# Second FFN stage: sums of blocks ahead of the other item's low part on VectorE, and 18 shared tiles

## The chip, the cores and the metric

One core of one Trainium2 chip runs the whole program. The time is device microseconds (us) of one execution; the kernel before takes 1112.65 us, the median of 3 runs (1112.34 to 1115.46).

## The reference

Sigmoid attention and a two-layer network behind it, in float32:

```python
scores = scale * np.matmul(q, k.transpose(0, 1, 3, 2)) - np.log(S)
attn = 1.0 / (1.0 + np.exp(-scores))
out = np.matmul(attn, v)              # 8 batches, 12 heads, 448 x 64
x = out.transpose(0, 2, 1, 3).reshape(B * S, H * D)      # 3584 x 768
h = x @ w_in                          # w_in 768 x 2048
g = np.maximum(0.01 * h, h)
return g @ w_out                      # w_out 2048 x 768
```

## The kernel before, in words

The program has three parts: attention, the first FFN product and the second FFN product. The change lies in the second product (`acc_*` on TensorE), and in the last slots of the first, where its work begins.

**Two parts for one number.** TensorE multiplies float32 numbers in a rounded form. So each operand is split: a high part (ScalarE copies it into the rounded type) and a low part (VectorE subtracts the high part from the whole). Three matmuls, high by high, high by low and low by high, stand for one product.

**Phases and items.** Tokens are worked in four phases p (two batches, 2 x 448 tokens each). The second product is a bilinear scheme: blocks of the activations g are combined, multiplied by combined blocks of w_out (20 "forms"), and the 20 products are summed up in 6 result tiles. The table `PRODUCTS` (line 41 on) has one entry for each product: its form of the weights, its accumulator chain in PSUM (A, B, D, E or C), its operand, and what is read out behind it. An operand such as `"30"` or `"01+30"` that the first stage has stored as a block of its own (`RAW`, `MADE`) is "single": it is loaded and split. One such as `"21-30"` that is not stored is a sum: both blocks are loaded, and VectorE adds or subtracts them. Singles are products 0, 2, 3, 4, 5, 7, 8, 10, 11 and 19, sums are 1, 6, 9 and 12 to 18. Each product is worked in two halves of two 128-row blocks: `items` has 4 x 20 x 2 = 160 entries (p, i, h). An item is 12 matmuls of 128 x 448. Within a phase, product i is items 2i and 2i + 1.

**Readouts.** `read` follows a product's second half: `"c10"` copies the accumulator to a new result tile (ScalarE), `"r11"`, `"+21"` and `"-00"` add it to or subtract it from a result tile or the other way round (VectorE). `!` marks the last change of a result, whose store to DRAM follows one slot later. A phase has 6 copies by ScalarE and 11 readouts by VectorE; two of these follow product 14.

**Order.** Each engine carries out its instructions in the order in which the program issues them (`pinned`). The program advances in slots: `slot(work)` first runs what was put off to this slot (`later`), then the work. In the second stage, slot k issues for VectorE and ScalarE the preparation of later items, and for TensorE the 12 matmuls of item k (the second of them is the first that reads the low part). Before the change, the order in slot k is: readouts of the product that ended with item k - 1 (k even) and stores that fell due; weights (`Wide`) that are loaded on the way, mainly in phase 0: 21 loads, each with a high part two slots later and a low part three slots later; then

```python
g_low(k + 1)      # VectorE: low part of item k+1
g_sum(k + 2)      # VectorE: sum of item k+2, over the block loaded last
g_high(k + 2)     # ScalarE: high part of item k+2
g_load(k + 4)     # SyncE: loads of item k+4
```

So on VectorE the sum of item k + 2 is followed directly by the low part of that same item (in slot k + 1), which reads what ScalarE makes out of the sum in between; where a readout falls due, it stands between them.

**Tiles.** Blocks are loaded into a ring of 6 tiles `g` (128 x 896 float32, 3.5 KB in a partition), high and low parts are made in a ring of 3 double tiles `gs`, results lie in a ring of 6 tiles `o`. An instruction that is the first to write a tile waits for whatever used that tile last. A block that two neighbouring products share is loaded once unless a sum has been written over it. Loads and stores are all issued by SyncE, in order.

Of the kernel before, what the change touches and what calls it, by code (L numbers as in the profile page):

```python
# [9 lines left out]
F32 = mybir.dt.float32  # L10
# [6 lines left out]
P = 128  # L17
# [6 lines left out]
PLACES = slice(1, 3), slice(3, 5), slice(5, 7), slice(0, 1)  # L24
ST = 10
AHEAD = 7
GG = 6

PACES = (4, 5, 4.2, 2.8, 2), 2.7
WAIT = 7  # L30
# [17 lines left out]
BLOCKS = "02", "01", "10", "00", "21", "03", "22", "11", "12", "13", "20", "23"  # L48
FORMS = 20
TRIPLES = tuple(range(i, min(i + 3, FORMS)) for i in range(0, FORMS, 3))  # L50
# [17 lines left out]
def attn_ffn_kernel(ctx: ExitStack, tc: tile.TileContext, qk, v, w_in, w_out, out):  # L68
# [41 lines left out]
    def sub(to, x, y):  # L110
        vec(out=to, in0=x, in1=y, op=ALU.subtract)
# [10 lines left out]
    def later(slots, *fns, first=False):  # L122

        chores.setdefault(now + slots, ([], []))[not first].extend(fns)

    def slot(work=None):
        nonlocal now
        for fns in chores.pop(now, ()):
            for fn in fns:
                fn()  # L130
        if work is not None:
            work()
        now += 1
# [644 lines left out]
        product(NQ - 1, first, k)  # L778
    right.close()
    KS = 2  # L780
    gp = ctx.enter_context(tc.tile_pool(name="gp", bufs=3, side="right", reuse_waits="tile"))
    shift(ctx, "pad2", 64, "right")
    t2a = ctx.enter_context(tc.tile_pool(name="t2a", bufs=AHEAD, side="right", reuse_waits="tile"))
    more = ExitStack()
    w1_stage.extend([more.enter_context(tc.tile_pool(name="stage2", bufs=4, side="right", reuse_waits="tile"))])

    items = [(p, i, h) for p in range(NQ) for i in range(FORMS) for h in range(2)]
    raw, gx, gs = {}, {}, {}

    def operand(x):  # L790

        fn = add if "+" in x else sub
        return (fn, *x.replace("-", "+").split("+"))

    def g_load(k):
        if k >= len(items):
            return
        p, i, h = items[k]
        x = PRODUCTS[i][2]
        names = [x] if x in gd[p] else operand(x)[1:]  # L800
        mine = []
        for n in names:
            if raw.get((p, n, h), -9) < k - 2:
                t = gp.tile([P, KS, S], F32, tag="g", name=f"g{n[:2]}_{p}_{i}_{h}", bufs=GG)
                dma(out=t, in_=gd[p][n][:, h * KS:h * KS + KS])
                raw[p, n, h], gx[p, n, h] = k, t
                mine.append(n)
        gs[k] = [None, mine[-1]]

    def g_sum(k):  # L810
        if k >= len(items):
            return
        p, i, h = items[k]
        x = PRODUCTS[i][2]
        gs[k][0] = gx[p, gs[k][1], h]
        if x not in gd[p]:
            fn, a, b = operand(x)
            fn(gs[k][0], gx[p, a, h], gx[p, b, h])
            del raw[p, gs[k][1], h]

    def g_high(k):
        if k < len(items):
            gs[k].append(gp.tile([P, 2, KS, S], F32R, tag="gs", name="gs{}_{}_{}".format(*items[k])))
            copy(out=gs[k][2][:, 0], in_=gs[k][0])

    def g_low(k):
        if k < len(items):
            sub(gs[k][2][:, 1], gs[k][0], gs[k][2][:, 0])

    use = [(g, u) for g in range(len(TRIPLES)) for u in range(KQ)]  # L830
    w2 = {(g, u): Wide(g, u, t2a, "t2") for g, u in use[:AHEAD]}
# [1 line left out]
    for k in range(NOP, size):  # L833
        m, at = divmod(k - NOP, 6)
        if m < AHEAD:
            x = w2[use[m]]
            if at == 1:
                later(0, x.load)
                later(3, x.high)
                later(4, x.low)  # L840
        rest = size - k
        if rest <= 4:
            later(0, lambda r=rest: g_load(4 - r))
        if rest == 2:
            later(0, lambda: g_sum(0), lambda: g_high(0))
        elif rest == 1:
            later(0, lambda: g_low(0), lambda: g_sum(1), lambda: g_high(1))
        slot(first.step)
    while chores:
        slot()  # L850
# [1 line left out]
    more.close()  # L852
    left.close()

    op = ctx.enter_context(tc.tile_pool(name="op", bufs=6, reuse_waits="tile"))
    t2b = ctx.enter_context(tc.tile_pool(name="t2b", bufs=len(use) - KQ - AHEAD - len(GROUPS), reuse_waits="tile"))
    for i, (g, u) in enumerate(use[AHEAD:]):
        small = len(TRIPLES[g]) < 3
        pool, tag = (ring, "ring") if i < len(GROUPS) else (t2b, "t1" if small else "t2")
        w2[g, u] = Wide(g, u, pool, tag, KQ if small else None)  # L860
# [6 lines left out]
    def place(p, o):  # L867
        m, t = int(o[0]), int(o[1])
        b = 2 * p + t
        return out[2 * m:2 * m + 2, :, b * S:(b + 1) * S]  # L870

    def store(p, o):
        dma(out=place(p, o).rearrange("m p s -> p m s"), in_=outs[p, o])

    def read(p, i):
        _, chain, _, reads = PRODUCTS[i]
        acc = accs[p, chain][:, :, :S]
        for x in reads:
            how, o = x[0], x[1:3]
            if how == "c":  # L880
                outs[p, o] = op.tile([P, 2, S], F32, tag="o", name=f"o{p}_{o}")
                copy(out=outs[p, o], in_=acc)
            else:
                t = outs[p, o]
                a, b = (acc, t) if how == "r" else (t, acc)
                (add if how == "+" else sub)(t, a, b)
            if x[3:]:
                later(1, lambda o=o: store(p, o))
# [5 lines left out]
    for k, (p, i, h) in enumerate(items):  # L894
        form, chain, _, reads = PRODUCTS[i]
        begins = h == 0 and firsts_at[chain] == i
        if begins:
            accs[p, chain] = psum("acc", f"acc{p}_{chain}")
        ending = k == len(items) - 1
        def work():  # L900
            for far, step in ((3, "low"), (2, "high"), (0, "load")):
                for x in loads.get(k - far, ()):
                    getattr(x, step)()
            g_low(k + 1)
            g_sum(k + 2)
            g_high(k + 2)
            g_load(k + 4)
            x = gs.pop(k)[2]
            g = form // 3
            for m in range(2):  # L910
                todo = [(e, part, n) for e in range(KS) for part, n in ((0, 0), (0, 1), (1, 0))]
                for at, (e, part, n) in enumerate(todo):
                    mm(accs[p, chain][:, m, :S], lhsT=w2[g, h * KS + e].of(form, part, m), rhs=x[:, n, e],
                       start=begins and at == 0, stop=h == 1 and at == len(todo) - 1, skip_group_check=True)
                if ending:

                    o, = (x[1:3] for x in reads)
                    t, acc, to = outs[p, o], accs[p, chain], place(p, o)
                    for cols, queue in zip(HALVES, (dma, dma_act)):
                        add(t[:, m, cols], t[:, m, cols], acc[:, m, cols])  # L920
                        queue(out=to[m, :, cols], in_=t[:, m, cols])

        slot(work)
        if h == 1 and not ending:
            later(0, lambda p=p, i=i: read(p, i))
    while chores:
        slot()
    ps.close()
# [42 lines left out]
```

## Time and profile before

| what | value |
|---|---|
| median of 3 runs | 1112.65 us |
| the profiled execution, its own time | 1114.31 us |
| its span, first to last instruction | 1112.5 us |
| granted TensorE clock, mean | 0.998 |
| TensorE busy (matmuls) | 1062.9 us, 96% |
| VectorE busy | 828.1 us, 74% |
| ScalarE busy | 607.1 us, 55% |
| moved by DMA | 298.61 MB, mean 268 GB/s |

Shares of the whole span hide what each part does. TensorE's matmuls overlap, and the ends of matmuls are modelled, so a busy share of 96% does not mean that it runs at its peak; how far apart matmuls start tells more. The chain of work that ended last puts 69% of the span on TensorE, 16% on VectorE, 6% on ScalarE and 6% on issuing. In the lines of the profile "idle before, releaser" is the time in which an engine stood still ahead of an instruction, and what ended it.

### The profile page before, as it was taken

Reading aid. Unit: us, or ns where it says so; the run is one execution under the profiler, and the core shown is the slowest. Engines: PE = TensorE matmul, PEld = TensorE weight load, DVE = VectorE, ACT = ScalarE, POOL = GpSimd, SP = SyncE. Lnnn points to the kernel's source line nnn. Section 1 sums busy time; section 2 is a strip of 40 time slices with the busy share of each in tenths; the row PEclk is TensorE's granted clock in tenths of the full one; section 3 lists DMA queues with packets and bytes.
Section 4 is the critical chain, followed back from the end, with each engine's and each line's share of the span. In section 5 each row is a group of like instructions: output and inputs, shape, how many; then the busy total and the mean of one; then the engine's idle time right before and its main releaser. Section 6 shows DMA issues by size and latency. Waiting matters only on the chain.

```text
span 1112.5 us, 16285 instructions
## 1 busy us (share of the span) xinstructions
PE 1062.9 (96%) x5786; PEld 867.3 (78%) x5786; DVE 828.1 (74%) x1187; ACT 607.1 (55%) x829; POOL 0.3 (0%) x5
## 2 busy tenths in 40 slices
PE   9999999999999999999999999979998899889987
PEld 5554555558999998998999988868886789678966
DVE  4778899777897889789675667887567756766675
ACT  6877877785556555655565546643442344334422
POOL 0000000000000000000000000000000000000000
PEclk9999999999999999999999999999999999999999
DMA  7878887897889798998887889888767876786675
GB/s 249 275 276 280 302 280 257 308 307 227 265 282 308 245 310 275 295 347 259 272 273 249 267 298 347 307 283 283 227 217 234 292 224 210 239 294 227 206 244 197
DMA packets 128000, 298.61 MB, mean 268 GB/s; under 512 B 13488, under 2 KB 66736, under 8 KB 127920
## 3 DMA queue, kind: packets, MB, share of 16 engines
q1 hardware_dynamic: 127200, 296.90, 80.0%
q8 instruction: 45, 0.74, 0.3%
q10 hardware_dynamic: 720, 0.69, 0.2%
q14 instruction: 35, 0.29, 0.1%
HBM read 210.89 MB, written 86.64 MB: 267 GB/s over the span
## 4 chain that ended last, share of the span: by engine, by line
PE 69%; DVE 16%; ACT 6%; issue 6%; DMA 1%; ACTq 0%; DVEq 0%; SPq 0%
PE px_h L103 18%; PE pv L103 11%; PE sc L103 10%; PE pz_h L103 9%; PE acc_A L103 8%; DVE g L103 7%; PE acc_B L103 6%; ACT gs L103 6%; DVE gs L103 5%; PE py_h L103 4%; PE acc_C L103 2%; DVE w L103 1%; DMA wx<-t 1%; DVE s L103 1%; PE acc_D L103 1%
## 5 line engine op out<-in xcount | busy, mean ns | idle before, releaser
L103 ACT CAST gs<-g 128x896 fp32r<-128x896 f32 x160 | 149.0, 942 | 242.0 <-DVE g L103 199.9
L103 DVE TENSOR_TENSOR gs<-g,gs 128x896 fp32r<-128x896 f32 x160 | 172.6, 1089 | 89.7 <-ACT gs L103 88.8
L103 PE MATMUL px_h<-hi,w 128*128 128x448 f32 x768 | 232.1, 363 | 3.0 <-DVE w L103 3.0
L103 PEld LDWEIGHTS px_h<-hi,w 128*128 128x128 f32 x768 | 143.3, 187 | 15.7 <-DVE w L103 5.5
L103 PE MATMUL px_h<-lo,w 128*128 128x448 f32 x384 | 139.1, 362 | 0.0
L103 PE MATMUL acc_B<-gs,w 128*128 128x448 f32 x576 | 122.2, 364 | 4.8 <-DVE gs L103 4.8
L103 PE MATMUL acc_A<-gs,w 128*128 128x448 f32 x576 | 121.6, 364 | 4.8 <-DVE gs L103 4.8
L103 ACT ACTIVATE s<-sc 128x896 f32<-128x896 f32 x144 | 119.5, 933 | 10.2 <-PE sc L103 10.2
L103 PEld LDWEIGHTS acc_B<-gs,w 128*128 128x128 f32 x576 | 107.1, 188 | 16.0 <-DVE gs L103 8.9
L103 PEld LDWEIGHTS acc_A<-gs,w 128*128 128x128 f32 x576 | 107.2, 187 | 15.4 <-DVE gs L103 8.2
L103 PE MATMUL pz_h<-hi,w 128*128 128x448 f32 x384 | 118.1, 362 | 0.0
L103 PE MATMUL pv<-s,v 128*64 128x448 f32 x576 | 114.0, 544 | 0.0
L103 DVE TENSOR_TENSOR w<-wx,w 128x768 fp32r<-128x768 f32 (+1 forms) x128 | 109.0, 853 | 6.2 <-ACT w L103 6.2
L103 PEld LDWEIGHTS sc<-qks 64*128 64x128 f32 x876 | 80.8, 189 | 24.1 <-issue 16.9
L103 PE MATMUL sc<-qks 64*128 64x448 f32 (+1 forms) x876 | 96.6, 371 | 0.5 <-DVE x L103 0.3
L103 ACT CAST w<-wx 128x768 fp32r<-128x768 f32 (+1 forms) x128 | 95.9, 750 | 0.3
L103 PEld LDWEIGHTS pv<-s,v 128*64 128x64 f32 x576 | 39.2, 137 | 64.2 <-issue 54.2
L103 DVE TENSOR_TENSOR g<-g,g 128x896 f32<-128x896 f32 x80 | 86.8, 1085 | 0.0
L103 PE MATMUL acc_D<-gs,w 128*128 128x448 f32 x288 | 67.5, 377 | 16.1 <-DVE gs L103 16.1
L103 ACT COPY c_h<-px_h 128x448 f32<-128x448 f32 x64 | 34.2, 534 | 89.0 <-PE px_h L103 79.9
L103 PEld LDWEIGHTS px_h<-lo,w 128*128 128x128 f32 x384 | 72.0, 188 | 4.8
L103 PEld LDWEIGHTS pz_h<-hi,w 128*128 128x128 f32 x384 | 72.0, 187 | 4.8
(61 smaller groups left out, 1323.1 us busy)
## 6 DMA issues: line engine op xcount, KB each, us to landing
g<-g SPq DMA_DIRECT2D x208, 448.0 KB, 4.2
wx<-t SPq DMA_DIRECT2D x96, 384.0 KB, 4.4
g<-c_h SPq DMA_DIRECT2D x128, 224.0 KB, 4.5
g<-s SPq DMA_DIRECT2D x96, 224.0 KB, 4.5
qk<-in_qk SPq DMA_DIRECT2D x46, 448.0 KB, 5.5
wr<-in_w_in SPq DMA_DIRECT2D x32, 384.0 KB, 3.3
wr<-in_w_out SPq DMA_DIRECT2D x32, 384.0 KB, 3.8
out<-o SPq DMA_DIRECT2D x23, 448.0 KB, 4.5
```

The source lines that it names most:

```text
L103: return lambda *args, **kw: tc.keep_in_program_order(issue(*args, **kw))
```

## The change

- **Order on VectorE.** In slot k the sum of item k + 2 now stands in front of the low part of item k + 1 (before: behind it); the high part of item k + 2 on ScalarE follows as before. Where a sum shares a block with the single product just before it (products 1 and 9), it is made one slot earlier still, since that single's low part is written over the block. Readouts move from the front of the slot behind the sums, the low parts and the weights.
- **Tiles.** Rings are given up. 18 tiles of one size (12 of `gp`, 6 of `op`) are handed out one by one from a list, the one given back longest ago first, for loaded blocks, sums, high parts and results alike. A low part is written over a loaded block of its own, a high part over the second one where there is one, else into a new tile. A sum gets a new tile, given back after the item's low part.
- **Loads.** An item is loaded when enough tiles are spare, up to 8 items ahead of the one whose matmuls were issued last (before: 4); `wanted` keeps tiles back for what the next slot needs. The loads of a slot are issued at its end. Product 16 is written `31+01`, and product 17 shares its block 31, so that a phase has 50 loads of blocks (before: 52).
- **Start.** The first item is loaded one slot earlier, and the sum of item 2 is made in the last slot of the first stage, in front of the low part of item 0.
- `op` now lies behind the weights `t2b` in memory.

```diff
--- before.py
+++ after.py
@@ -24,7 +24,7 @@
 PLACES = slice(1, 3), slice(3, 5), slice(5, 7), slice(0, 1)
 ST = 10
 AHEAD = 7
-GG = 6
+GG, OO, FAR = 12, 6, 8
 
 PACES = (4, 5, 4.2, 2.8, 2), 2.7
 WAIT = 7
@@ -44,7 +44,7 @@
     (4, "A", "01", ("r21",)), (5, "B", "10-21", ("c01",)), (6, "A", "10+01", ("c20",)), (7, "B", "21-20", ("c00",)),
     (8, "A", "10", ("r00",)), (9, "B", "20-10", ()), (10, "A", "11-10", ("r01",)), (11, "B", "00+30", ("r10!",)),
     (12, "D", "01-00", ("-00!",)), (13, "E", "11+01", ()), (14, "C", "30-31", ("-01!", "-21")), (15, "D", "30-20", ()),
-    (17, "C", "01+31", ()), (19, "E", "21-31", ("+21!",)), (18, "D", "10+00", ("-20!",)), (16, "C", "11-21", ("+11!",)))
+    (17, "C", "31+01", ()), (19, "E", "21-31", ("+21!",)), (18, "D", "10+00", ("-20!",)), (16, "C", "11-21", ("+11!",)))
 BLOCKS = "02", "01", "10", "00", "21", "03", "22", "11", "12", "13", "20", "23"
 FORMS = 20
 TRIPLES = tuple(range(i, min(i + 3, FORMS)) for i in range(0, FORMS, 3))
@@ -778,54 +778,116 @@
         product(NQ - 1, first, k)
     right.close()
     KS = 2
-    gp = ctx.enter_context(tc.tile_pool(name="gp", bufs=3, side="right", reuse_waits="tile"))
+    gp = ctx.enter_context(tc.tile_pool(name="gp", bufs=1, side="right", reuse_waits="tile"))
     shift(ctx, "pad2", 64, "right")
     t2a = ctx.enter_context(tc.tile_pool(name="t2a", bufs=AHEAD, side="right", reuse_waits="tile"))
     more = ExitStack()
     w1_stage.extend([more.enter_context(tc.tile_pool(name="stage2", bufs=4, side="right", reuse_waits="tile"))])
 
     items = [(p, i, h) for p in range(NQ) for i in range(FORMS) for h in range(2)]
...
+    spare, homes = [(gp, f"g{n}") for n in range(GG)], {}
+
+    def grab(name, dtype=F32R):
+
+        pool, tag = spare.pop(0)
+        t = pool.tile([P, KS, S], dtype, tag=tag, name=name)
+        homes[id(t)] = pool, tag
+        return t
+
+    def drop(t):
+        spare.append(homes.pop(id(t)))
+
+    class Operand:
+
+        def __init__(self, k):
+            self.k = k
+            self.p, self.i, self.h = items[k]
+            x = PRODUCTS[self.i][2]
+            self.single = x in gd[self.p]
+            self.names = [x] if self.single else x.replace("-", "+").split("+")
+            self.fn = add if "+" in x else sub
+            self.before = operands[k - 2] if self.i else None
+            self.shared = [n for n in self.names if self.before and n in self.before.new] if not self.single else []
+            self.new = [n for n in self.names if n not in self.shared]
+            self.lent, self.made, self.hi, self.ready = (), None, None, False
+            if self.before:
+                self.before.lent = self.shared
+
+        def label(self, what):
+            return f"{what}_{self.p}_{self.i}_{self.h}"
+
+        def load(self):
+            self.raw = {}
+            for n in self.new:
+                t = self.raw[n] = grab(self.label(f"g{n[:2]}"))
+                dma(out=t.bitcast(F32), in_=gd[self.p][n][:, self.h * KS:self.h * KS + KS])
+
+        def first(self):
+
+            return self.before and self.before.single and self.shared
+
+        def whole(self):
+            if self.ready:
+                return
+            self.ready = True
+            if self.single:
+                self.lo, = self.raw.values()
+                self.x = self.lo.bitcast(F32)
+                return
+            a, b = (self.before.raw[n] if n in self.shared else self.raw[n] for n in self.names)
+            self.made = self.x = grab(self.label("gf"), F32)
+            self.fn(self.made, a.bitcast(F32), b.bitcast(F32))
+            if self.shared and not self.before.single:
+                for n in self.shared:
+                    drop(self.before.raw[n])
+            own = [t for n, t in self.raw.items() if n not in self.lent]
+            self.lo = own.pop()
+            self.hi = own.pop() if own else None
+
+        def high(self):
+            if self.hi is None:
+                self.hi = grab(self.label("gh"))
+            copy(out=self.hi, in_=self.x)
+
+        def low(self):
+            sub(self.lo, self.x, self.hi)
+            if self.made is not None:
+                drop(self.made)
+
+        def done(self):
+            drop(self.hi)
+            drop(self.lo)
+
+    operands = []
+    for k in range(len(items)):
+        operands.append(Operand(k))
+    ahead = 0
+
+    def wanted(k):
+
+        n = 0
+        for j in (k + 2, k + 3):
+            x = operands[min(j, len(items) - 1)]
+            n += not x.single and (j == k + 2 or bool(x.first())) and not x.ready
+        x = operands[min(k + 2, len(items) - 1)]
+        n += x.single or len([m for m in x.new if m not in x.lent]) < 2
+        if k and k % 2 == 0:
+            n += sum(y[0] == "c" for y in PRODUCTS[items[k - 1][1]][3])
+        return n
+
+    def g_load(k, far):
+
+        nonlocal ahead
+        while ahead <= min(far, len(items) - 1) and len(spare) >= len(operands[ahead].new) + wanted(k + 1):
+            operands[ahead].load()
+            ahead += 1
+
+    def g_step(k, step):
         if k < len(items):
-            gs[k].append(gp.tile([P, 2, KS, S], F32R, tag="gs", name="gs{}_{}_{}".format(*items[k])))
-            copy(out=gs[k][2][:, 0], in_=gs[k][0])
-
-    def g_low(k):
-        if k < len(items):
-            sub(gs[k][2][:, 1], gs[k][0], gs[k][2][:, 0])
+            getattr(operands[k], step)()
 
     use = [(g, u) for g in range(len(TRIPLES)) for u in range(KQ)]
     w2 = {(g, u): Wide(g, u, t2a, "t2") for g, u in use[:AHEAD]}
@@ -839,12 +901,10 @@
                 later(3, x.high)
                 later(4, x.low)
         rest = size - k
-        if rest <= 4:
-            later(0, lambda r=rest: g_load(4 - r))
-        if rest == 2:
-            later(0, lambda: g_sum(0), lambda: g_high(0))
-        elif rest == 1:
-            later(0, lambda: g_low(0), lambda: g_sum(1), lambda: g_high(1))
+        if rest <= 5:
+            later(0, lambda r=rest: g_load(-r, 5 - r))
+        for at, what in {2: ((0, "whole"), (0, "high")), 1: ((2, "whole"), (1, "whole"), (0, "low"), (1, "high"))}.get(rest, ()):
+            later(0, lambda at=at, what=what: g_step(at, what))
         slot(first.step)
     while chores:
         slot()
@@ -852,8 +912,10 @@
     more.close()
     left.close()
 
-    op = ctx.enter_context(tc.tile_pool(name="op", bufs=6, reuse_waits="tile"))
     t2b = ctx.enter_context(tc.tile_pool(name="t2b", bufs=len(use) - KQ - AHEAD - len(GROUPS), reuse_waits="tile"))
+    shift(ctx, "pad3", 64)
+    op = ctx.enter_context(tc.tile_pool(name="op", bufs=1, reuse_waits="tile"))
+    spare.extend((op, f"o{n}") for n in range(OO))
     for i, (g, u) in enumerate(use[AHEAD:]):
         small = len(TRIPLES[g]) < 3
         pool, tag = (ring, "ring") if i < len(GROUPS) else (t2b, "t1" if small else "t2")
@@ -870,7 +932,9 @@
         return out[2 * m:2 * m + 2, :, b * S:(b + 1) * S]
 
     def store(p, o):
-        dma(out=place(p, o).rearrange("m p s -> p m s"), in_=outs[p, o])
+        t = outs.pop((p, o))
+        dma(out=place(p, o).rearrange("m p s -> p m s"), in_=t)
+        drop(t)
 
     def read(p, i):
         _, chain, _, reads = PRODUCTS[i]
@@ -878,7 +942,7 @@
         for x in reads:
             how, o = x[0], x[1:3]
             if how == "c":
-                outs[p, o] = op.tile([P, 2, S], F32, tag="o", name=f"o{p}_{o}")
+                outs[p, o] = grab(f"o{p}_{o}", F32)
                 copy(out=outs[p, o], in_=acc)
             else:
                 t = outs[p, o]
@@ -898,19 +962,20 @@
             accs[p, chain] = psum("acc", f"acc{p}_{chain}")
         ending = k == len(items) - 1
         def work():
+            early = k + 3 < len(items) and bool(operands[k + 3].first())
+            for far, step in ((3, "whole"),) * early + ((2, "whole"), (1, "low"), (2, "high")):
+                g_step(k + far, step)
             for far, step in ((3, "low"), (2, "high"), (0, "load")):
                 for x in loads.get(k - far, ()):
                     getattr(x, step)()
-            g_low(k + 1)
-            g_sum(k + 2)
-            g_high(k + 2)
-            g_load(k + 4)
-            x = gs.pop(k)[2]
+            if k % 2 == 0 and k:
+                read(*items[k - 1][:2])
+            me = operands[k]
             g = form // 3
             for m in range(2):
                 todo = [(e, part, n) for e in range(KS) for part, n in ((0, 0), (0, 1), (1, 0))]
                 for at, (e, part, n) in enumerate(todo):
-                    mm(accs[p, chain][:, m, :S], lhsT=w2[g, h * KS + e].of(form, part, m), rhs=x[:, n, e],
+                    mm(accs[p, chain][:, m, :S], lhsT=w2[g, h * KS + e].of(form, part, m), rhs=(me.hi, me.lo)[n][:, e],
                        start=begins and at == 0, stop=h == 1 and at == len(todo) - 1, skip_group_check=True)
                 if ending:
 
@@ -920,9 +985,10 @@
                         add(t[:, m, cols], t[:, m, cols], acc[:, m, cols])
                         queue(out=to[m, :, cols], in_=t[:, m, cols])
 
+            me.done()
+            g_load(k, k + FAR)
+
         slot(work)
-        if h == 1 and not ending:
-            later(0, lambda p=p, i=i: read(p, i))
     while chores:
         slot()
     ps.close()
```

More of the change, by code (lines that the diff above doesn't have):

```diff
@@ L787, in attn_ffn_kernel @@
     items = [(p, i, h) for p in range(NQ) for i in range(FORMS) for h in range(2)]
[L788 to L821, printed above, removed]
-        if k < len(items):
-            gs[k].append(gp.tile([P, 2, KS, S], F32R, tag="gs", name="gs{}_{}_{}".format(*items[k])))
-            copy(out=gs[k][2][:, 0], in_=gs[k][0])
```

## The prediction

> **What bounds the kernel now.** I read the page first, then the waits of one phase of the second FFN stage, then the timelines of TensorE and VectorE in it. An "item" is one of the 160 half products of that stage (12 matmuls each, 40 items to a phase, 4 phases); I number items within their phase, and "slot k" is the program's step that issues item k's matmuls. The waits of the third phase (span from 887 to 997 us):
>
> ```profile
> span 1112.5 us, 16285 instructions
> ```
> ```profile
> ACT gs L103 <- DVE g L103: 50.6, 19, 4.7
> DVE gs L103 <- ACT gs L103: 25.5, 24, 2.1
> ```
>
> ScalarE waits for VectorE's sums (g), and VectorE's low parts (gs) wait for ScalarE's high parts: 24 times, 25.5 us. The two engines pass one item back and forth. What it costs TensorE is read from where each phase's first matmul starts (start, length, tile, count):
>
> ```profile
> 660.59 2.76 PE L103 MATMUL acc_A<-gs,w 128*128 128x448 f32 x13
> ...
> 776.38 3.96 PE L103 MATMUL acc_A<-gs,w 128*128 128x448 f32 x19
> ...
> 886.83 3.36 PE L103 MATMUL acc_A<-gs,w 128*128 128x448 f32 x16
> ```
> ```profile
> 947.27 0.36 PE L103 MATMUL acc_D<-gs,w 128*128 128x448 f32 x1
> 948.00 2.67 PE L103 MATMUL acc_D<-gs,w 128*128 128x448 f32 x12 [0.37 <-DVE gs L103]
> 951.17 2.47 PE L103 MATMUL acc_D<-gs,w 128*128 128x448 f32 x11 [0.51 <-DVE gs L103]
> 953.49 0.37 PE L103 MATMUL acc_E<-gs,w 128*128 128x448 f32 x1
> ...
> 992.47 4.96 PE L103 MATMUL acc_C<-gs,w 128*128 128x448 f32 x24
> 997.26 0.96 PE L103 MATMUL acc_A<-gs,w 128*128 128x448 f32 x4
> ```
>
> Unhindered, 24 matmuls take 997.26 - 992.47 = 4.8, so an item takes 2.40 and a phase 96.0. Phase 0 takes 776.38 - 660.59 = 115.8 (19.8 lost), phase 1 110.45 and phase 2 110.43 (14.4 lost each); phase 3 runs the same program on the same sizes, so 14.4 too. Together 63.0 us are lost: the most that this edit can win, 1049.6 for the median. Most of it lies in items 24 to 37, whose operands are sums: 992.47 - 947.27 = 45.2 for 14 items that need 33.6. The same place on VectorE:
>
> ```profile
> 944.67 1.09 DVE L103 TENSOR_TENSOR g<-g,g 128x896 f32<-128x896 f32 x1
> 946.85 1.09 DVE L103 TENSOR_TENSOR gs<-g,gs 128x896 fp32r<-128x896 f32 x1 [1.09 <-ACT gs L103]
> 947.86 1.08 DVE L103 TENSOR_TENSOR g<-g,g 128x896 f32<-128x896 f32 x1
> 948.86 1.08 DVE L103 TENSOR_TENSOR o<-acc_B,o 128x896 f32<-128x896 f32 x1
> 950.03 1.09 DVE L103 TENSOR_TENSOR gs<-g,gs 128x896 fp32r<-128x896 f32 x1
> 951.04 1.08 DVE L103 TENSOR_TENSOR g<-g,g 128x896 f32<-128x896 f32 x1
> ...
> 967.95 2.08 DVE L103 TENSOR_TENSOR o<-o,acc_C 128x896 f32<-128x896 f32 x2
> ...
> 992.66 1.09 DVE L103 TENSOR_TENSOR o<-o,acc_D 128x896 f32<-128x896 f32 x1 [1.57 <-PE acc_D L103]
> ```
>
> Sum, 1.09 idle for ScalarE, low, next sum: 947.86 - 944.67 = 3.19 per item, against TensorE's 2.40. The reads (o) hide in the idle time. Five prices follow for what comes: VectorE's operations start 1.00 apart (967.95: two in 2.08); low may start 2.18 after its own sum (946.85 - 944.67); the item's second matmul, the first that needs the low part, comes 1.15 after low's start (948.00 - 946.85); after a late second matmul the next item starts 2.32 later instead of 2.20 (953.49 - 951.17), 0.12 extra; what item j held is free 0.2 after item j+1 starts (992.66 against 992.47).
>
> **The change: the order.** Slot k on VectorE is now sum k+2, low k+1, then reads. Between sum k+2 and low k+2 stand low k+1 and sum k+3, 2.0 of work plus reads, so ScalarE's 2.18 is nearly always covered; the 3.19 falls to 2.00 without reads. The stall does not all go, since VectorE is then nearly full: in slots 22 to 33 it has 24 sums and lows and 5 reads, 29.0 against 12 x 2.40 = 28.8. And sums now write into fresh tiles: by following the list of spare tiles through the code, sums 24, 25, 28, 31, 33, 34, 35 and 36 get a tile that the item three before held (sum k+2 after item k-1), so VectorE cannot run ahead there.
>
> **The change: the shared tiles.** SyncE's queue issues stores and loads in order, and a tile handed on is waited for:
>
> ```profile
> SPq L103 <- DVE gs L103: 187.9, 96, 4.4
> ```
>
> That is the present wait of loads for lows. New is that three loads in each phase get a tile that held a result: item 29's second block gets that of result 10 (stored in slot 25, just ahead of it in the queue), item 32's second that of 00 (slot 27), item 37's first that of 01 (slot 31). Each must wait until the store has landed, and all behind it waits too. Ahead of item 29 the lookahead is shortest (4 items). No row shows a load held by a store; its price is bounded below by nothing (if the load is not held) and above by the longest landings. The issues with their medians to landing, from four stretches: a store with loads behind it, a quiet one, a store at a double read, and the crowded start of the stage:
>
> ```profile
> g<-g SPq DMA_DIRECT2D x3, 448.0 KB, 4.0
> out<-o SPq DMA_DIRECT2D x1, 448.0 KB, 2.9
> ```
> ```profile
> g<-g SPq DMA_DIRECT2D x3, 448.0 KB, 3.3
> ```
> ```profile
> out<-o SPq DMA_DIRECT2D x1, 448.0 KB, 5.2
> ```
> ```profile
> g<-g SPq DMA_DIRECT2D x8, 448.0 KB, 8.3
> ```
>
> I take 2.9 and 3.3, as the queue has run empty by slot 25 (no load is issued in slots 21 to 23). [...]
>
> **Phases 1 to 3, walked through** (zero: item 22's first matmul; a transfer queued behind another lands 1.1 later, an estimate from 4.0 against 2.9). Slot 22: sum 24 at 0.2, low 23, read (r01) at 2.2. Slot 23: sum 25 at 3.2, low 24 at 4.2, second matmul 5.35 instead of 5.0: 0.35 + 0.12 lost, 0.5. Slot 24: sum 26 at 5.2, low 25, read (r10) 7.2 to 8.3. Slot 25: sum 27, low 26 at 9.2, 0.1 late: 0.2 lost. The store of 10 is issued at 8.4 and lands at 11.3; then item 29's second load is issued and lands at 14.6. Slot 26: sum 28 at 10.2, low 27, read to 13.3. Slot 27: sum 29 could start at 13.3 and starts at 14.7; low 28, behind it, at 15.7, second matmul 16.85, where 15.25 was due: 1.6 + 0.12, 1.7 lost, with TensorE standing 1.8. Loads 30 and 31 land one by one about 1.1 later each, in time. Item 32's second load waits for the store of 00, which lands behind load 31 at about 17.9, and comes at 21.3, when VectorE is just there. Slot 30 has two reads, so low 32 starts at 26.4, its matmul is due at 26.55 and comes at 27.55: 1.1 lost. Item 37's load comes at 32.4, sum 37 starts at 34.4: nothing. Sum: 0.5 + 0.2 + 1.7 + 1.1 = 3.5 of stall for 14.4: 10.9 won, in three phases 32.7.
>
> **Phase 0** has weights as well. A low of weights takes 0.87 on VectorE:
>
> ```profile
> 688.79 0.95 DVE L103 TENSOR_TENSOR w<-w 128x768 fp32r<-128x768 f32 x1
> 689.66 1.08 DVE L103 TENSOR_TENSOR gs<-g,gs 128x896 fp32r<-128x896 f32 x1
> ```
>
> In slots 22 to 33 there are four of them, and four of two thirds the size (0.6, an estimate): 5.9 on top of 29.0, so 34.9 against 28.8, 6.1 lost; the held load adds about 1.2: 7.3. The start of the stage on VectorE:
>
> ```profile
> 659.53 1.08 DVE L103 TENSOR_TENSOR gs<-g,gs 128x896 fp32r<-128x896 f32 x1
> 660.53 0.62 DVE L103 TENSOR_TENSOR s<-c_h,c_h 128x448 f32<-128x448 f32 x1
> 661.83 1.70 DVE L103 TENSOR_TENSOR s<-c_h,c_h 128x448 f32<-128x448 f32 x3 [0.69 <-ACT c_h L103]
> 663.44 1.08 DVE L103 TENSOR_TENSOR gs<-g,gs 128x896 fp32r<-128x896 f32 x1
> ```
>
> Sum 2 now stands in front of low 0 (1.0 late for the first item), sum 3 and the late sums s in front of low 1 (1.75 late): 2.75; the stalls of items 2 and 3 go. Loads of four items at once in slot 0 stand ahead of weights in the crowded queue, each 1.1 of transfer: about 1.0, an estimate, by head-of-queue waits on ScalarE (none to 3 by the 8.3 above). Sum 7.3 + 2.75 + 1.0 = 11.1 for 19.8: 8.7 won.
>
> **Hidden, at nothing.** Two loads fewer in each phase (items 34 and 35 share block 31 with 32 and 33): outside phase 0 the queue was not what ended a wait last. Early sums (items 2, 3, 18, 19): slots 15 to 18 and 38 to 41 hold seven and eight operations of 1.00 in 9.6; if that cover were gone, each would cost its 1.00. Reads come behind sum and low, up to 2.0 later: accumulator A or B is written again 4.8 after its item ended, the read ends at 3.3. ScalarE's copies gain from free time: its high parts have two slots.
>
> Total: 32.7 + 8.7 = 41.4. The profiled execution (1114.31, of it 1112.5 span) would become 1072.9, span 1071.1; it lies 1.66 over the median 1112.65, which becomes **1071.2**.
>
> **Rivals.** *Loads in time* (not held by the store, or landing early): item 28 loses about 0.2 instead of 1.7, so 2.0 per phase; phase 0 loses 9.9 instead of 11.1: 1112.65 - 3 x 12.4 - 9.9 = **1065.6**. For it: one load only is decisive. Against: the code's order.
>
> *Half clock.* Where TensorE stood in phase 0, its clock fell:
>
> ```profile
> 750.19 3.75 PE L103 MATMUL acc_D<-gs,w 128*128 128x448 f32 x11 [1.92 <-DVE gs L103]
> 753.74 5.35 PE L103 MATMUL acc_C<-gs,w 128*128 128x448 f32 x24
> ```
> ```profile
> 752.00:756.00 4.00, 4.00 (x16) 3.59 (x15) 2.70 (x3) 1.65 (x3) 0.00 (x0) 0.69 0.97 358
> ```
>
> The granted clock is 0.69 there. From 750.19 to 753.74 it took 3.55 for 2.32, and the next 24 matmuls 0.39 more: 1.6 lost. The change gathers the stall into one gap of 1.8 at item 28; if each brings this, 1.6 more in each of four phases, 6.4: **1077.6**. [...]
>
> *Loads later.* Store 5.2 and load 4.1 or more: item 29's load 3 later, item 32's 1 to 2, with half clock: 5.6 more per phase: **1088**.
>
> *Slower.* The same held loads at the crowded landing of 8.3: item 29's at 8.4 + 8.3 + 8.3 = 25, 10.4 later, item 32's some 8.5 later again: 18.9 more per phase, **1128**. This decides from 10.9 more stall per phase and 8.7 in phase 0, landings of some 6.5 each. Against: 8.3 was seen only where weights filled the queue.
>
> *No change*: the tiles tie VectorE to TensorE so closely that 3.19 stays: **1112.6**. Against: 2.00 of work and a 0.2 release per slot.
>
> **Numbers.** Forecast 0.54, in time 0.20, half clock 0.11, later 0.10, slower 0.03, none 0.02. The forecast's own bounds are 1066 to 1077 (weights 0 to 3, held load ±0.5 in each phase). The range is 1062 to 1085: it takes in the first two rivals with the same bounds and leaves out the slower, the unchanged and most of "later". A difference under 0.3% cannot be told from none. Faster 0.95, same 0.02, slower 0.03.
>
> **What would show it.** Right: on VectorE sums directly before lows with no idle in items 2, 3, 12 and 13; waits of SyncE's queue for the DMA of out, about 3 us, three per phase; one gap of TensorE near 1.8 at item 28 and one near 1 at item 32; phases 1 to 3 near 99.5, phase 0 near 107. Wrong: low parts still waiting for ScalarE; gaps at other items; sums waiting for loads beyond 29; phases over 104.

## The result and the profile after

The median after is 1084.65 us (4 runs, 1081.94 to 1085.95), before 1112.68 (4 runs): ratio 0.974, 95% interval 0.9714 to 0.9765, so 28.0 us (2.5%) faster. The profiled execution of after took 1081.94, the shortest of the four. The chain of work that ended last, by engine, from the page of before, and then span and chain from the page of after:

```profile
PE 69%; DVE 16%; ACT 6%; issue 6%; DMA 1%; ACTq 0%; DVEq 0%; SPq 0%
```
```profile
span 1080.1 us, 16340 instructions
...
PE 80%; DVE 8%; DMA 8%; issue 2%; SPq 0%; ACT 0%; DVEq 0%; ACTq 0%
```

TensorE's share of the chain rises from 69% to 80%, VectorE's falls from 16% to 8% and ScalarE's from 6% to nothing; that of DMA rises from 1% to 8%. Waits of the third phase (870 to 972 us) in after: who waits, for what, us in total, times, longest.

```profile
ACT gh L103 <- DVE gf L103: 29.5, 13, 4.5
DVE g L103 <- ACT gh L103: 13.3, 11, 2.1
ACT g L103 <- DVE gf L103: 8.9, 4, 2.6
...
DVE gf L103 <- DMA g<-g: 4.3, 4, 2.1
```

The first three lines are the hand-over between the two engines. The low parts' wait for ScalarE is halved (25.5 before). ScalarE's wait for sums now has two lines, as its high parts go to a new tile (gh) or over a loaded block (g): together 38.4, for 50.6 before. The last line is new: sums that wait for a load. The first matmul of each phase, after:

```profile
658.46 0.37 PE L103 MATMUL acc_A<-gh,w 128*128 128x448 f32 x1
...
767.49 0.36 PE L103 MATMUL acc_A<-gh,w 128*128 128x448 f32 x1
...
869.61 0.36 PE L103 MATMUL acc_A<-gh,w 128*128 128x448 f32 x1
...
972.38 0.36 PE L103 MATMUL acc_A<-gh,w 128*128 128x448 f32 x1
```

| us | phase 0 | 1 | 2 | 3 (to the start of its last matmul, and 0.20 for that one) |
|---|---|---|---|---|
| before | 115.79 | 110.45 | 110.43 | 111.49 |
| after | 109.03 | 102.12 | 102.77 | 103.95 |
| won | 6.8 | 8.3 | 7.7 | 7.5 |
| forecast | 8.7 | 10.9 | 10.9 | 10.9 |

That is 30.3 in the stage for the 41.4 forecast. The other 2.1 of the two profiled executions (1114.31 - 1081.94 = 32.4) lie ahead of the stage (660.59 against 658.46). By the matmuls of both traces they are there 84 us after the start (83.73 against 81.57 for the same matmul), in attention, which was not edited; so they are hardly the change's.

What is left sits at item 28. TensorE in phase 2 of after, whose item 22 starts at 922.41 (the zero of the walk): first and second matmul of items 24 and 28.

```profile
927.21 0.37 PE L103 MATMUL acc_D<-gh,w 128*128 128x448 f32 x1
927.76 0.47 PE L103 MATMUL acc_D<-g,w 128*128 128x448 f32 x1 [0.19 <-DVE g L103]
...
937.61 0.37 PE L103 MATMUL acc_C<-gh,w 128*128 128x448 f32 x1
...
940.17 0.47 PE L103 MATMUL acc_C<-g,w 128*128 128x448 f32 x1 [2.20 <-DVE g L103]
```

VectorE there (gf is a sum, g a low part), and the same stretch of SyncE's queue (first with neighbouring loads in one row, then from 934 on):

```profile
928.75 1.08 DVE L103 TENSOR_TENSOR g<-gf,gh 128x896 fp32r<-128x896 f32 x1
929.76 1.08 DVE L103 TENSOR_TENSOR o<-acc_B,o 128x896 f32<-128x896 f32 x1
930.76 1.08 DVE L103 TENSOR_TENSOR gf<-g,g 128x896 f32<-128x896 f32 x1
...
938.02 1.09 DVE L103 TENSOR_TENSOR gf<-g,g 128x896 f32<-128x896 f32 x1 [2.14 <-DMA g<-g]
939.03 1.08 DVE L103 TENSOR_TENSOR g<-gf,gh 128x896 fp32r<-128x896 f32 x1
...
960.72 1.09 DVE L103 TENSOR_TENSOR gf<-g,g 128x896 f32<-128x896 f32 x1 [1.03 <-DMA g<-g]
```
```profile
930.87 0.39 SPq L103 DMA_DIRECT2D out<-o  x1
931.35 5.10 SPq L103 DMA_DIRECT2D g<-g  x4
936.54 0.39 SPq L103 DMA_DIRECT2D out<-o  x1
```
```profile
934.47 1.98 SPq L103 DMA_DIRECT2D g<-g  x3
```

The store of result 10 goes out at 930.87. Of the four loads behind it the first, item 29's first block, goes out at 931.35; the second, item 29's second block, waits until 934.47. Sum 29 waits 2.14 us for it, low 28 stands behind sum 29, and TensorE stands 2.20. The chain of waits runs through the two next held loads:

```profile
936.54 6.51 DMA out<-o
...
943.12 3.29 DMA g<-g
...
946.53 1.09 DVE gf L103
...
949.65 6.35 DMA out<-o
...
956.43 4.17 DMA g<-g
```

The first of these two held loads goes out 0.07 us after the store has landed (943.05), the second 0.02 us after (the row at 956.43 is the load behind it, which had to wait too). All nine held loads of phases 1 to 3 go out 0.02 to 0.07 us after a landing. The clock behind the gap (busy time of PE, PEld, DVE, ACT, POOL, then granted clock, DMA share, GB/s):

```profile
938.00:942.00 4.00, 1.83 (x8) 1.69 (x9) 3.78 (x4) 1.42 (x2) 0.00 (x0) 0.95 0.87 278
942.00:946.00 4.00, 4.00 (x14) 3.61 (x14) 2.50 (x3) 1.41 (x2) 0.00 (x0) 0.62 0.71 264
```

3.41 us at half clock followed the long gap in every phase (item 28 in phases 1 to 3, item 32 in phase 0).

### The profile page after: what moved, and what is told of

Read it like the earlier page. It is cut to its first block, busy times and chain, and to the rows that moved or that the text cites. A ratio compares the mean times of both kernels' runs of the same rounds, so it can differ in the third digit from the quotient of the medians.

```text
span 1080.1 us, 16340 instructions
## 1 busy us (share of the span) xinstructions
PE 1052.3 (97%) x5786; PEld 874.3 (81%) x5786; DVE 827.7 (77%) x1187; ACT 608.0 (56%) x829; POOL 0.3 (0%) x5
## 4 chain that ended last, share of the span: by engine, by line
PE 80%; DVE 8%; DMA 8%; issue 2%; SPq 0%; ACT 0%; DVEq 0%; ACTq 0%
PE px_h L103 19%; PE pv L103 12%; PE sc L103 11%; PE acc_A L103 10%; PE pz_h L103 10%; PE acc_B L103 9%; PE py_h L103 5%; DMA out<-o 4%; DMA g<-g 3%; PE acc_C L103 3%; DVE g L103 2%; PE acc_D L103 2%; DVE gf L103 2%; DVE o L103 1%; DVE w L103 1%
## 5 line engine op out<-in xcount | busy, mean ns | idle before, releaser
L103 ACT CAST gh<-gf 128x896 fp32r<-128x896 f32 x64 | 60.3, 942 | 112.0 <-DVE gf L103 100.4
L103 DVE TENSOR_TENSOR gf<-g,g 128x896 f32<-128x896 f32 x80 | 87.1, 1089 | 37.5 <-PE acc_A L103 16.1
L103 DVE TENSOR_TENSOR g<-g,gh 128x896 fp32r<-128x896 f32 x80 | 86.5, 1089 | 36.9 <-ACT gh L103 35.4
L103 PE MATMUL acc_B<-gh,w 128*128 128x448 f32 x384 | 112.1, 362 | 0.0
L103 ACT CAST gh<-g 128x896 fp32r<-128x896 f32 x80 | 74.9, 942 | 54.5 <-PE acc_B L103 22.2
L103 PE MATMUL acc_A<-gh,w 128*128 128x448 f32 x320 | 93.4, 362 | 0.0
L103 PE MATMUL acc_A<-g,w 128*128 128x448 f32 x256 | 78.1, 362 | 2.6 <-DVE g L103 2.6
L103 PEld LDWEIGHTS acc_B<-gh,w 128*128 128x128 f32 x384 | 72.0, 187 | 4.9
L103 DVE TENSOR_TENSOR g<-gf,gh 128x896 fp32r<-128x896 f32 x64 | 69.4, 1086 | 8.5 <-ACT gh L103 8.5
```

The costliest lines, as they stand in the source:

```text
L103: return lambda *args, **kw: tc.keep_in_program_order(issue(*args, **kw))
```

## The experiments

**Theory.** Sum before low, with readouts behind, wins the time; the shared tiles give part of it back, because a load gets the tile of a result just stored. **Rivals**: the free tiles win it and the order alone does little; readouts or half clock account for it. In what follows, an item's loss is the time from its first matmul to the next item's, less 2.40, in the profiled execution.

**1, the order with readouts behind, without the new tiles**, on the kernel before with its rings:

```diff
+            g_sum(k + 2)
+            g_low(k + 1)
+            g_high(k + 2)
             for far, step in ((3, "low"), (2, "high"), (0, "load")):
...
-            g_low(k + 1)
-            g_sum(k + 2)
-            g_high(k + 2)
+            if k % 2 == 0 and k:
+                read(*items[k - 1][:2])
             g_load(k + 4)
...
-        if h == 1 and not ending:
-            later(0, lambda p=p, i=i: read(p, i))
```

> The kernel before with the new order alone: in each slot of the second stage the sum of item k+2, the low part of item k+1, the weights' low part, then the readouts; the old rings of 6 g, 3 gs and 6 o tiles stay, loads stay 4 items ahead. Theory (what the changed kernel has left, 6 to 7 us of stall in each of phases 1 to 3, comes from loads held by stores of results, and from the half clock that the gap at item 28 brings): here no load can be held by a store, so only VectorE's fullness is left, about 2 to 4 us per phase: 1066 to 1077 us, no gap over 1.5 us at item 28, clock 1.00. Rival (the shared tiles and the longer lookahead are what makes the new order pay; with 6 tiles the loads of sums come late): 1085 to 1105 us, sums waiting for the DMA of g in items 24 to 37.

Measured 1073.87 (1072.03 to 1076.45), ratio 0.9645 (0.962 to 0.9671); phases 108.7, 100.5, 99.6, 100.8. Item 28 in phase 2, first and second matmul:

```profile
935.87 0.37 PE L103 MATMUL acc_C<-gs,w 128*128 128x448 f32 x1
936.78 4.87 PE L103 MATMUL acc_C<-gs,w 128*128 128x448 f32 x23 [0.55 <-DVE gs L103]
```

In phases 1 to 3 the clock stays full, item 28 loses 0.35 to 0.83, item 32 1.6 and item 34 0.85 to 1.37, somewhat more than the 2 to 4 us per phase expected; in phase 0 there is half clock behind item 1, and item 28's gap is 2.64, against the expectation. The order with the readouts behind wins 38.8 us; the rest of the change loses about 11 of that again.

**2, the tiles with the old order**, on the kernel after:

```diff
-            for far, step in ((3, "whole"),) * early + ((2, "whole"), (1, "low"), (2, "high")):
+            for far, step in ((3, "whole"),) * early + ((1, "low"), (2, "whole"), (2, "high")):
```

> The changed kernel with the old order on VectorE: low part of item k+1 in front of the sum of item k+2 (the two early sums per phase stay early); tiles, lookahead and readouts as changed. Theory: the hand-over between VectorE and ScalarE is the whole gain, so it comes back, 3.2 us per item of sums, and held loads come on top: 1108 to 1120 us. Rival (tiles and lookahead gain by themselves): 1095 us or less.

Measured 1091.62 (1090.31 to 1092.92), ratio 0.9805 (0.9788 to 0.9822). The theory missed: it left out that this kernel keeps its readouts behind. In phases 1 to 3, items 27 to 37 still lose 0.7 to 0.8 each (item 29 up to 1.04, item 31 1.47), as the hand-over must; the losses of items 2, 3, 12, 13, 24 and 25 are gone. Runs 5 and 6 follow from this.

**3, a stored tile given back three slots later**, on the kernel after:

```diff
-        drop(t)
+        later(3, lambda: drop(t))
```

> The changed kernel, but a result's tile goes back to the list three slots after its store is issued, so that no load right behind the store gets it; 18 tiles as before, lookahead up to one item shorter. Theory (held loads and the half clock behind the gap): the wait of the load queue for out falls from about 4.5 us per load to under 1, TensorE's gap at item 28 from 2.3 us to under 0.6, the clock stays at 1.00 there, phases 1 to 3 take 98 to 99.5 us for 102.1 to 103: 1071 to 1077 us. Rival (lookahead is simply too short there, whoever had the tile): the gap at item 28 stays, 1082 to 1087 us.

Measured 1076.65 (1073.44 to 1081.18), ratio 0.9674 (0.9644 to 0.9703); phases 108.9, 101.0, 99.9, 101.3. SyncE's queue no longer waits for a store, and the clock stays full in phases 1 to 3. By the medians this wins 8.0 us. But the gap of item 28 stays, against the expectation of under 0.6: from matmul to matmul it is 2.65, 1.72 and 2.01 us in phases 1 to 3, where after has 2.47, 2.56 and 2.49. Items 28 and 29 together lose 6.1 in these phases and 12.1 in after; in phase 1 2.57 for 3.97, with a gap no shorter. So most of what is won at item 28 goes with the half clock. How the 8.0 divides between held loads and half clock is not shown. VectorE in phase 2 (item 22 at 922.8):

```profile
937.55 1.09 DVE L103 TENSOR_TENSOR gf<-g,g 128x896 f32<-128x896 f32 x1 [1.34 <-DMA g<-g]
```

Sum 29 is still late by 1.34, though its load no longer waits for a store. SyncE's queue waits for TensorE and VectorE to be done with tiles (138.1 and 96.6 us in phases 1 to 3), so the loads' short lookahead is the likely cause; it was not tested. Item 28 keeps a loss of 1.6 to 2.6.

**4, TensorE kept at work ahead of item 28**, on the kernel after: in phases 1 to 3 eight more matmuls, into the accumulator that item 28 starts anew.

```diff
+            for _ in range(8 * (p > 0 and i == 14 and h == 0)):
+                mm(accs[p, chain][:, 0, :S], lhsT=w2[g, 0].of(form, 0, 0), rhs=me.hi[:, 0], start=True, stop=True,
+                   skip_group_check=True)
```

> The changed kernel with 8 matmuls more ahead of item 28 in phases 1 to 3 (1.6 us of TensorE at 0.2 us each, into the accumulator that the item's first matmul clears); they fall into the gap of 2.3 us in which TensorE waits for item 28's low part. Theory (standing still over about 2 us brings the half clock for 3.4 us): the granted clock stays at 1.00 there and items 28 and 29 get 1.0 to 1.7 us shorter in each of the three phases: 1079 to 1082 us. Rival (the clock falls for another reason, or its fall costs nothing as VectorE is late anyway): the same within 1 us as the changed kernel, 1084 to 1086 us.

Measured 1082.3 (1079.51 to 1083.3), ratio 0.9717 (0.9698 to 0.9737), overlapping the interval of after. Window and TensorE's row behind the gap, phase 2:

```profile
942.00:946.00 4.00, 2.99 (x14) 2.48 (x15) 2.56 (x3) 0.94 (x1) 0.00 (x0) 1.00 0.68 263
```
```profile
941.91 0.47 PE L103 MATMUL acc_C<-g,w 128*128 128x448 f32 x1 [1.18 <-DVE g L103]
...
945.59 0.47 PE L103 MATMUL acc_C<-g,w 128*128 128x448 f32 x1 [1.01 <-DVE g L103]
```

The clock stays at 1.00, but TensorE stands 1.18 and, right after, 1.01 instead: with or without half clock the loads behind the store are late. In phase 1 items 28 and 29 lose 2.6 instead of 4.0, as expected, but items 31 and 32 lose 2.3 instead of 0.8, and phases 1 to 3 together take as long as in after. So the half clock costs some 1.4 us where it falls, and what is left of that at the end of a phase lies between nothing and 1.4; these runs do not settle it.

**5, readouts behind, old order**, on the kernel before: run 1 without its exchange of sum and low.

> The kernel before with one thing moved: the readouts stand behind low part, sum, and the weights' low part in each slot instead of at its front; old order of low part and sum, old rings. Theory (a readout at the front of a slot waits for TensorE's previous item and holds the low part and the sum behind it; moved, VectorE runs a slot ahead, and the hand-over costs nothing until that lead is used up): no stall at items 2, 3, 12, 13, 24 and 25, 0.7 to 0.8 each from about item 27 to 37, phases 1 to 3 at 104 to 106 us: 1087 to 1096 us. Rival (what the old order gained in the new tiles came from the tiles and the longer lookahead): 1105 us or more.

Measured 1091.93 (1091.85 to 1094.79), ratio 0.9816 (0.9801 to 0.9831), as run 2. VectorE in phase 1:

```profile
831.65 1.08 DVE L103 TENSOR_TENSOR g<-g,g 128x896 f32<-128x896 f32 x1
...
833.82 1.09 DVE L103 TENSOR_TENSOR gs<-g,gs 128x896 fp32r<-128x896 f32 x1 [1.08 <-ACT gs L103]
```

The hand-over is untouched (low 2.17 after its sum, 1.08 idle), and yet 21 us are won. The edit also puts the weights' parts behind low and sum; phases 1 to 3, which have no weights, win 5.3, 5.3 and 5.0, so the readouts do it there, and only for the 5.5 of phase 0 are the two not told apart.

**6, the order, readouts still in front**, on the kernel before: `g_sum(k + 2)` put ahead of `g_low(k + 1)`, nothing else.

> The kernel before with the sum of item k+2 ahead of the low part of item k+1, but the readouts still at the front of the slot; old rings. Theory: where a readout falls due in a slot with a sum, the low part starts 2.2 us behind the item's start instead of by 1.46: 0.86 lost at items 11 or 12, 23, 25, 27 and 1.9 at 31, about 5 to 6 per phase with late loads: 1076 to 1090 us. Rival (the place of the readouts is of no account once the hand-over is covered): as the order with the readouts behind, 1072 to 1076 us.

Measured 1097.16 (1093.06 to 1098.65), ratio 0.9845 (0.9824 to 0.9865). VectorE and TensorE in phase 1, at the start of item 25:

```profile
834.23 1.09 DVE L103 TENSOR_TENSOR o<-acc_B,o 128x896 f32<-128x896 f32 x1 [0.56 <-PE acc_B L103]
835.24 1.08 DVE L103 TENSOR_TENSOR g<-g,g 128x896 f32<-128x896 f32 x1
836.24 1.09 DVE L103 TENSOR_TENSOR gs<-g,gs 128x896 fp32r<-128x896 f32 x1
```
```profile
837.38 2.47 PE L103 MATMUL acc_D<-gs,w 128*128 128x448 f32 x11 [0.58 <-DVE gs L103]
```

The readout waits 0.56 for the product to end; sum and low stand behind it and come 2.0 later, and TensorE loses 0.86 at items 1, 11, 23, 25 and 27 and 1.86 at 31 (two readouts). The price per slot was hit; the total lies outside the 1076 to 1090 expected, since items 28 and 34 and phase 0 lost as well. In the old rings, then: before 1112.96, readouts behind 1091.93, order 1097.16, both 1073.87.

**7 and 10, a readout out of the full stretch**: run 1 with the readout of product 11 put off to slot 37, and product 16 written as in the change.

```diff
-    (17, "C", "01+31", ()), ...
+    (17, "C", "31+01", ()), ...
...
+            if k % 2 == 0 and k and items[k - 1][1] != 11:
                 read(*items[k - 1][:2])
+            if k % 40 == 37:
+                read(p, 11)
```

> The new order with the readouts behind and the old rings; the readout of product 11 (its accumulator is not written again before the next phase) put off from slot 24 to slot 37, its store with it, and product 16 written so that product 17 shares its block 31 (two loads fewer per phase). Theory (in items 24 to 37 VectorE is full and the queue's loads come late by the transfers ahead of them): one VectorE operation and three transfers less there: phases 1 to 3 at 97.5 to 99.5 us, gap at item 28 under 0.4, none at item 34; item 32 still 1 to 1.6: 1066 to 1071 us. Rival (the lookahead of 4 items is what is late): the gaps at items 28 and 34 stay, 1072 to 1075 us.

> The same kernel as e7_late_readout, for a comparison on the same chip: 1067 to 1070 us, item 32 losing 1.6 in every phase.

Measured 1068.61 (1067.83 to 1072.1), ratio 0.9606 (0.9589 to 0.9624), and again 1068.97, ratio 0.9598 (0.958 to 0.9615). In phases 1 to 3 item 28 loses at most 0.2 and item 34 nothing, as expected. Phase 3 took 101.4 for the 97.5 to 99.5 expected, with 0.85 and 0.60 lost at items 1 and 2; and in run 10 item 32 lost 1.57, 0.78 and 1.60, not 1.6 in every phase. This version has the lowest median, with the old rings; the interval of run 7 touches that of run 1.

**8, the same readout put off in the kernel of run 3.**

> The changed kernel with result tiles put back three slots late and the readout of product 11 put off to slot 37. Theory: as for the old rings, the store and one VectorE operation leave the crowded stretch, but one tile more is held there; gap at item 28 under 1.2 instead of 1.6 to 2.6, phases 1 to 3 at 98 to 100 us: 1069 to 1075 us. Rival (the shared list is short of tiles there, so the tile held longer costs lookahead): no better than with late return alone, 1076 us or more.

Measured 1072.28 (1071.48 to 1073.63), ratio 0.9635 (0.962 to 0.9649). Item 28 loses 0.6 to 1.2 in phases 1 to 3. The interval overlaps that of run 3, so the gain over it is likely and not shown.

**9, the old order in slot 31 alone**, in the kernel of run 7, against the loss of 1.6 at item 32.

```diff
-            g_sum(k + 2)
-            g_low(k + 1)
+            for step, far in ((g_low, 1), (g_sum, 2))[::1 if k % 40 == 31 else -1]:
+                step(k + far)
```

> The order with the late readout of product 11 and the shared block 31, and in slot 31 alone the old order of low part and sum: behind the two readouts of product 14 the high part of item 32 is long done, so low 32 need not stand behind sum 33. Theory (the new order pays only where ScalarE's high part is not ready; behind two readouts it puts 1.0 us of sum in front of the late low part): item 32 loses 0.5 to 0.7 instead of 1.6 in every phase, item 33 at most 0.2: 1063 to 1066 us. Rival (VectorE is full there, so the operation is only late one item later): items 33 or 34 lose what item 32 gains, 1067 to 1070 us.

Measured 1070.24 (1066.46 to 1071.28), ratio 0.9604 (0.9586 to 0.9621), against 0.9598 for run 10 beside it: no gain. In phases 1 to 3 item 32 falls to 0.4 to 0.6, and item 33, which lost nothing in run 10, loses 0.8: the loss moves on by an item, as the rival has it.

## Why the prediction was right, and where it missed

- **Direction and places: right; the mechanism in part.** The hand-over between sum and low cost what was read from the rows, and the order takes it away, but it was not the only bound: the place of the readouts was one too (below). In phases 1 to 3 of after, the main losses lie at items 24, 26, 28 and 32, as walked through; item 24 lost 0.46 to 0.47 (0.5 forecast), 26 lost 0.33 (0.2), 32 from 0.8 to 1.6 (1.1). Items 2, 3 and 13 lose nothing, item 12 only 0.29 and in phase 0. The lows that still wait for ScalarE (13.3 us) all start by 918.6, before item 22, where TensorE does not wait for them. Of the signs named for being wrong this one came, without a price, and another with one: sums 32 and 37 wait for loads.
- **The held load: right, its size was not.** Zero to store 8.46 (8.4 forecast), store to landing 3.6 (2.9), sum 29 at 15.6 (14.7). The gap at item 28 was 2.56 from matmul to matmul for the 1.8 forecast, and half clock followed: items 28 and 29 together lost 4.1 in phase 2, where 1.7 stood. That is the term that was mis-sized. The *half clock* rival (0.11) came true along with the forecast's mechanism, though by run 4 late loads would have taken at least part of its price anyway. So did half of *loads later* (0.10): item 32's second load landed at 24.0 for the 21.3 forecast, and 1084.65 lies nearer to that rival's 1088 than to the forecast.
- **The next stores: missed.** The queue was taken to be quiet. Stores with loads in flight took 6.5 and 6.35 to land, so item 37's load was late too (sum 37 waits 1.03) and item 36 lost 0.5 to 0.6 in phases 1 and 2, where "nothing" stood. In phase 3, where the last of these stores took 4.7, item 36 lost nothing. Waits of SyncE's queue from phase 1 on:

```profile
SPq L103 <- DMA out<-o: 40.2, 9, 6.0
```

  Three per phase, as named, but 4.5 us each and not 3.
- **Phase 0**: 13.0 lost for 11.1. The start cost 3.14 (1.27 and 1.87 at items 0 and 1) for 2.75; at item 32 the half clock lay.
- **"Reads come behind sum and low ... at nothing": wrong as an attribution.** The prediction had the reads hide in the idle time and gave the whole gain to the exchange of sum and low. By runs 5 and 6 the place of the readouts alone is worth 21 us, the exchange alone 16, both 39. A readout waits for a product's last matmul (0.56 us in the rows of run 6), and in front of the slot it keeps sum and low, which come 2.0 later there, from running ahead. The direction came out since the change does both, and the walk through phases 1 to 3 has the readouts behind, as the change has them.
- **What the tiles cost**: about 11 us by run 1 against after, 8.0 of it undone by run 3. The rest (2.8) has overlapping runs; the short lookahead at item 29 and sums tied to fresh tiles are argued, not shown. More tiles were not tried, and neither were the new start and the new place of `op` by themselves.
- **The sum.** 13.4 over the forecast: 11.1 in the stage as above, less 2.1 won ahead of it, and 4.4 because the profiled execution of before lay 1.7 above its median and that of after 2.7 below. The result lies inside the range by 0.35: 28.0 us came of the 41.4 forecast, and it was the width of the range that held, with luck, and not the sum.

## What to carry to other kernels

On an engine that works in order, an operation that waits for another engine's late result (here a readout of an accumulator) belongs behind what others are waiting for, and moving it can be worth more than the exchange that one was looking at (21 us against 16 here). When tiles are handed out from one list, the tile of a store just issued should not go to the next load: in the kernel after, such a load waited in the queue until the store had landed (nine times, 4.5 us on average), and all loads behind it waited too; giving the tile back three slots later won 8.0 us. To judge such a change, build its parts separately; the order without the tiles was better than both together (1073.87 against 1084.65).

## What was unexpected of the hardware

TensorE's clock fell to one half for 3.41 us behind gaps, from matmul to matmul, of 2.13 to 2.60 us (2.29 in phase 0 of before; 2.13 in phase 0 and 2.47 to 2.56 in phases 1 to 3 of after; 2.60 at item 1 of phase 0 in runs 6 and 10). It stayed full behind one of 2.60 at the same place in run 7, behind one of 2.65 in phase 1 of run 3 and behind this one in phase 0 of run 1 (2.64):

```profile
731.66 0.36 PE L103 MATMUL acc_C<-gs,w 128*128 128x448 f32 x1
734.30 1.88 PE L103 MATMUL acc_C<-gs,w 128*128 128x448 f32 x8 [2.28 <-DVE gs L103]
```

The granted clock (third from the end) with item 28's gap in phase 2 of after and behind it, and then with the gap of run 1:

```profile
938.19:941.60 3.41, 1.43 (x7) 1.34 (x8) 3.21 (x4) 1.02 (x2) 0.00 (x0) 1.00 0.84 261
941.60:945.01 3.41, 3.41 (x11) 3.04 (x10) 2.32 (x3) 1.24 (x2) 0.00 (x0) 0.50 0.68 247
```
```profile
729.17:732.58 3.41, 2.68 (x12) 2.17 (x12) 1.55 (x3) 0.90 (x2) 0.00 (x0) 1.00 1.01 369
732.58:736.00 3.42, 1.70 (x8) 1.61 (x9) 3.42 (x4) 1.46 (x2) 0.00 (x0) 1.00 1.00 316
```

So in these runs the length of the gap alone does not decide; what else counts was not tested.

A store of 448 KB landed after 2.6 us with no other transfer in flight (the last ones of after), 2.9 with one transfer ahead of it (before), 3.6 ahead of item 29's held load, and 4.7 to 6.5 with three to five transfers in flight (the stores ahead of the held loads of items 32 and 37 in phases 1 to 3 of after).
